# A rewritten issue order for a one-core attention and two-layer MoE kernel

## The chip, the cores and the metric

The kernel runs on one core of a Trainium2 chip. The metric is the device time of one execution in microseconds; the value used for comparison is the median of several runs. The profile comes from one execution of its own, whose span (first to last instruction) is a little shorter than its device time.

## The reference

The computation has three stages, all in float32:

```
attention: B=2, H=8, S=768, D=64; bucket = 6 sign bits of x @ proj (64x6)
  scores = (q @ k.T) / 8 where the buckets of q and k agree, else -1e9
  attn   = softmax(scores);  x = attn @ v, heads side by side -> 1536 x 512
MoE 1:  h = x @ w_in (512x2048);  g = s * relu(h)^2 + b;  x = g @ w_out (2048x512)
MoE 2:  a = x @ w1, b = x @ w2 (512x1024 each);  h = (a * b) @ w3;  out = h @ w_out
```

## The kernel before

Every float32 operand is split into a high and a low part of a faster format, so each product is three matrix multiplications (high x high, low x high, high x low). Weights are brought in as 64-bit words and converted by six steps each, `conv0` to `conv5` (lines 257 to 271): `conv0`, `conv1` and `conv3` on VectorE, `conv2` and `conv4` on ScalarE or GpSimd, `conv5` on GpSimd or VectorE.

Attention works on 16 heads, each in three units of 256 query rows. A unit is two `score` operations (line 529, four matmuls each), for each a `max` on VectorE (line 543) and an `exp` on ScalarE (line 551), three `turn` operations that transpose the result on TensorE (line 565), a split of each transposed piece into high and low parts (`hi` on ScalarE line 603, `lo` on VectorE line 607; for the middle piece `out`, `phi`, `plo` on ScalarE and GpSimd, lines 586 to 597), and three `pv` operations (lines 571 and 572). Per head two `bits` operations (line 492) and `mask` operations (line 510) build the bucket operands, and several small DMAs move halves of the operands between partitions (`mq_d` for the first head, line 477). The first head's second score operation group needs the landed `mq_d`.

MoE 1 runs in two batches: as soon as batch 0's attention is done its `h` and `o` products (line 759) are interleaved with the attention of batch 1, then batch 1's own products follow. The second batch reads its converted weights back from DRAM (`again_wi`, `again_wo`, line 747). While MoE 1 runs, the last two matrices of MoE 2 are multiplied together (`fold`, line 1162). MoE 2 forms its two products by a seven-product scheme (p1 to p7 per block, line 759; `cadd`, `c1`, line 1132 and 1137, combine them on VectorE and ScalarE), multiplies them (`times`, line 1187), splits the result (`abh` on ScalarE line 1190, `cl` on VectorE or GpSimd line 1191) and multiplies by the folded matrix (`share`, line 1203). Twelve output tiles are copied (`ya`, `yv`) and written out.

The order of all this is not left to loops. The program first describes 3773 operations in a `Plan` (each with one or more ways to be done on some engine, and with the tiles it reads and writes) and then issues them in an order written out as a string. `emit` takes three constants: `ORDER` names, two letters each, which operation is issued next; `WAYS` gives for each of 509 operations that can run on two or three engines which one it uses; `PLACES` gives for each of 1724 tiles in which of its pool's buffers it lies. Each engine, and the queue of SyncE that issues all DMAs, executes its own operations strictly in the order in which they stand in `ORDER`. A tile that takes over a buffer has to wait until the operations on the tile before it in that buffer are done. The microseconds written at each `plan.op` are not used by `emit`.

```
        for o in self.ops:
            o["engine"], o["us"], o["fn"] = o["ways"][int(next(ways)) if len(o["ways"]) > 1 else 0]
        issued = [
            self.ops[64 * LETTERS.index(ORDER[2 * i]) + LETTERS.index(ORDER[2 * i + 1])] for i in range(len(ORDER) // 2)
        ]
...
        for o in issued:
            o["fn"]()
```

Of the kernel before, what the change touches and what calls it, by code (L numbers as in the profile page):

```python
# [18 lines left out]
B, H, S, D = 2, 8, 768, 64  # L19
# [10 lines left out]
U = 256  # L30
# [29 lines left out]
    "IuYKIzJ+JaIfKAJeIDI3J/JbL/JiI8JyKBI4MAMGJuJjMFKjJfI5JkKCJcKkJgO2MBJvI9KmJwKlIgJhYcKnJ3MHIEJzLAKhMCKoIFJlLBMD"  # L60
    "J0IjKDJmMIIhMELDJ4J1I+JnLCKMJ5JxMJKiLEKHL9KEJ2KIIiKFLfLFIkO4J6KJMKLgKtK4J7KKLiKNJ8KpKuLjKGNPLVI/KyKqKOKLNXJA"
    "LkNVKPYdJBK5LGKrKQMNLhKvK6KRLKK7NQLWKsMOKzMQNWLLK0LPMPKwQGMRNRYLLHMiNSMLMSKxLIMMK1LMMjNTK2MlLNLQNYLXNULlLYMk"
    "K3LpL0LRQIK8LJLqMmLOLmNZLSLrNNYWLuLTNaM3LnLsMnLUMcM4LZLoYXMdM6LvYOYDMTM5MeO5LtLwMXK9MUPAM7LxMYO6MxNbL1MsLyMV"
    "NdM8L2LzYsK+L3NeLaMZYtO/MtNgK/PBNfMWMaNhO7MyN6LbL4O8NcYPMbMzMfMuLcN7MoMgO9MvMpMhYuNiO+PCYvLdMqNGN8YQN9YYNBYw"
    "MrL5NCYRYxMwL6PEN+M0LeNHPDM9NDM1OZNIYSN/M2NnOaNsM+NEOcaUNoTAM/ObNjYeNANFNyOdNtL7NJNkOEQJNuNpPHNKNlNqQROJOeNL"
    "O3OANzQQNmPIOFQKPKOKN0NrPJOLNvPLOGOjRwNwQLX7YZOkNxN1PcOBQMOHYkPMOCQPQNPdPFODOPOfPGQOPePfaVOIOgaWOMPgYlOlONYm"
    "QSRyOQOoRxOOPxOhYaOpN2YnYfOROqOSPWPhOmPyOiQTY0YoQHP0YyOuYpQUPXOnYgYqPNPYOTRzOrYzPRYhacYrY1R7PSN3Y2OvYiPOY8P1"
    "PzY3Y9PPPTY4QXP2R0Y5Y+OwOxY6ZEOsQ0Y7aMN4Y/R6QVOtQYZFOUZAZGaXZBZHOyQZPUQ1PQXrPrZCZMR5ZIadZNPsZDZOPtZPZJQaZQaN"
    "OzR1ZRPmQbQWPVPnPZR2N5ZUPaaOPiR3aePjZVaPPoR4ZWZSPkPpR9ZXOXPbR8QcZcV6ZkZTQ2ZdaQZlQsZYZeZKZZZmaRaYZfQAZLaZPlaS"
    "RTQBaaakZnZgQCafQ3ZhOYasZuagR+P7O0ZoPqahRUP8PuP9P3Q4ZvRVP+ZpZqQ5alZraiZwP4ZsPvP5OVZxa0ZtOWRWYjTCO1QmQtTDPwZz"  # L70
    "amZ0TKTEZyP6ZaRXZ1QnQhQoZ2anQiUqP/aTZ3ZiQdYTatQjQDaoZ9QeZbZ+apa1Z4auSBaqQfavZ5QEaCR/Zja8Z/SCSAajZ6UrZ7TJSDaD"
# [1192 lines left out]
```

## Time and profile before

| what | us |
|---|---|
| median of 3 runs | 741.59 (741.3 to 741.89) |
| the profiled execution: device time | 742.74 |
| the profiled execution: span | 740.9 |
| TensorE busy (PE), weight loads (PEld) | 729.0, 694.6 |
| VectorE (DVE), ScalarE (ACT), GpSimd (POOL) busy | 590.8, 393.2, 297.5 |

The engines are named PE (TensorE, with PEld for its weight loads), DVE (VectorE), ACT (ScalarE), POOL (GpSimd) and SP (SyncE, which issues the DMAs here). Busy time is the sum of an engine's instructions. Matmul ends are modelled, so how long PE was held up is read better from the starts of its instructions than from its busy time.

### The profile page before, as it was taken

Reading aid. Unit: us, or ns where it says so; the run is one execution under the profiler, and the core shown is the slowest. Engines: PE = TensorE matmul, PEld = TensorE weight load, DVE = VectorE, ACT = ScalarE, POOL = GpSimd, SP = SyncE. Lnnn points to the kernel's source line nnn. Section 1 sums busy time; section 2 is a strip of 40 time slices with the busy share of each in tenths; the row PEclk is TensorE's granted clock in tenths of the full one; section 3 lists DMA queues with packets and bytes.
Section 4 is the critical chain, followed back from the end, with each engine's and each line's share of the span. In section 5 each row is a group of like instructions: output and inputs, shape, how many; then the busy total and the mean of one; then the engine's idle time right before and its main releaser. Section 6 shows DMA issues by size and latency. Waiting matters only on the chain.

```text
span 740.9 us, 12707 instructions
## 1 busy us (share of the span) xinstructions
PE 729.0 (98%) x4356; PEld 694.6 (94%) x4356; DVE 590.8 (80%) x1133; ACT 393.2 (53%) x778; POOL 297.5 (40%) x322
## 2 busy tenths in 40 slices
PE   8899999999999999999999999999999999999997
PEld 6889999999999999999999998999998999999996
DVE  7999999999889889999898667665998965664542
ACT  6989989987667667665373432433533312311111
POOL 2698989886565564334230311032125200111000
PEclk9999999999999999999999999999999999999999
DMA  7856557566677477347888996788899998475502
GB/s 217 244 132 175 141 160 194 149 181 171 195 228 236 119 232 255 93 133 254 288 267 298 317 312 242 256 274 290 315 338 315 353 312 261 141 240 186 179 22 86
DMA packets 78592, 163.03 MB, mean 220 GB/s; under 512 B 8896, under 2 KB 46272, under 8 KB 78528
## 3 DMA queue, kind: packets, MB, share of 16 engines
q1 hardware_dynamic: 78528, 162.22, 68.5%
q8 instruction: 35, 0.57, 0.3%
q14 instruction: 29, 0.24, 0.1%
HBM read 103.09 MB, written 41.21 MB: 195 GB/s over the span
## 4 chain that ended last, share of the span: by engine, by line
PE 86%; DVE 7%; DMA 3%; ACT 2%; issue 1%; SPq 0%; DVEq 0%; ACTq 0%
PE x L759 18%; PE h L759 15%; PE p L759 15%; PE y L1203 9%; PE t L565 7%; PE sc L529 7%; PE psw L1162 6%; PE o L571 4%; PE o L572 4%; PE bits L492 2%; DVE sc L543 1%; DVE pt L607 1%; DMA t<-in_qkT 1%; DMA q<-mm 1%; DMA rd<-rq 1%
## 5 line engine op out<-in xcount | busy, mean ns | idle before, releaser
L759 PE MATMUL h<-x,w_wi 128*128 128x384 f32 x768 | 148.1, 338 | 0.0
L759 PE MATMUL x<-g,w_wo 128*128 128x384 f32 x768 | 146.9, 337 | 1.0 <-DVE rl L833 0.9
L759 PEld LDWEIGHTS x<-g,w_wo 128*128 128x128 f32 x768 | 133.6, 188 | 3.6 <-DVE rl L833 1.6
L759 PEld LDWEIGHTS h<-x,w_wi 128*128 128x128 f32 x768 | 133.6, 188 | 2.5 <-DVE pt L607 0.2
L1132 DVE TENSOR_TENSOR c<-c,p 128x384 f32<-128x384 f32 x112 | 60.2, 552 | 57.7 <-PE p L759 54.4
L543 DVE TENSOR_SCALAR_CACHE_REDUCE sc<-sc 128x768 f32<-128x768 f32 x96 | 91.6, 957 | 3.4 <-PE sc L529 2.4
L551 ACT ACTIVATE p<-sc,least 128x768 f32<-128x768 f32 x96 | 86.9, 906 | 11.1 <-DVE sc L543 7.7
L529 PE MATMUL sc<-k,q 128*128 128x384 f32 x384 | 87.0, 347 | 3.0 <-ACT p L551 2.0
L565 PE MATMUL t<-ident,p 128*128 128x128 f32 x576 | 83.9, 273 | 0.2
L759 PE MATMUL p<-x,w 128*128 128x384 f32 x384 | 77.5, 337 | 0.4 <-DVE c L1132 0.3
L571 PE MATMUL o<-pt,vv 128*128 128x256 f32 x288 | 76.9, 295 | 0.1
L572 PE MATMUL o<-pt,vv 128*128 128x256 f32 x288 | 73.1, 282 | 0.0
L565 PEld LDWEIGHTS t<-ident,p 128*128 128x128 f32 x576 | 67.9, 140 | 5.3 <-DVE pt L607 1.5
L759 PEld LDWEIGHTS p<-x,w 128*128 128x128 f32 x384 | 68.0, 188 | 4.5 <-DVE c L1132 1.3
L597 POOL TENSOR_TENSOR pt<-pf,pt 128x512 fp32r<-128x512 f32 x48 | 63.2, 1317 | 21.6 <-ACT pt L593 20.7
L607 DVE TENSOR_TENSOR pt<-t,pt 128x512 fp32r<-128x512 f32 x96 | 65.0, 683 | 6.7 <-ACT pt L603 5.5
L529 PEld LDWEIGHTS sc<-k,q 128*128 128x128 f32 x384 | 64.4, 188 | 5.2 <-ACT p L551 3.0
L603 ACT CAST pt<-t 128x512 fp32r<-128x512 f32 x96 | 56.0, 586 | 16.7 <-PE t L565 7.6
L571 PEld LDWEIGHTS o<-pt,vv 128*128 128x128 f32 x288 | 54.4, 189 | 0.8 <-DVE xf L624 0.3
L572 PEld LDWEIGHTS o<-pt,vv 128*128 128x128 f32 x288 | 54.5, 189 | 0.2
L838 ACT ACTIVATE g<-rl,b_bc 128x384 fp32r<-128x384 f32 x64 | 38.9, 615 | 25.5 <-PE x L759 17.4
L1162 PE MATMUL psw<-w_wo,w_w 128*128 128x512 f32 x192 | 51.6, 394 | 0.0
(263 smaller groups left out, 1271.7 us busy)
## 6 DMA issues: line engine op xcount, KB each, us to landing
w<-kept_s SPq DMA_DIRECT2D x64, 256.0 KB
kept_wo<-w_wo SPq DMA_DIRECT2D x24, 512.0 KB
w_wo<-kept_wo SPq DMA_DIRECT2D x24, 512.0 KB
w<-kept_a SPq DMA_DIRECT2D x48, 256.0 KB
raw_wi<-in_w_in SPq DMA_DIRECT2D x16, 512.0 KB
raw_wo<-in_w_out SPq DMA_DIRECT2D x16, 512.0 KB
kept_wi<-w_wi SPq DMA_DIRECT2D x16, 512.0 KB
raw_w_a<-in_w SPq DMA_DIRECT2D x16, 512.0 KB
```

The costliest lines, as they stand in the source:

```text
L529: nc.tensor.matmul(sc()[:, i, :HALF], x[:, t], y[:, i * HALF : (i + 1) * HALF], start=st, stop=not st)
L543: lambda j=j, sc=sc: nc.vector.tensor_scalar(sc()[:, :, :HALF], sc()[:, :, :HALF], OUT, None, ALU.min, ALU.min, accum_out=least()[:, j : j ...
L551: lambda j=j, k=k, sc=sc: nc.scalar.activation(ps[j](), sc()[:, :, :HALF], AF.Exp, bias=least()[:, j : j + 1], scale=-1.0, accum_out=ssum( ...
L565: nc.tensor.transpose(tp()[:, e, j * P : (j + 1) * P], flat[:, c * P : (c + 1) * P], ident)
L571: nc.tensor.matmul(o()[:, :U], w, pt()[:, 0, e], start=(c == 0), stop=False)
L572: nc.tensor.matmul(o()[:, :U], w, pt()[:, 1, e], start=False, stop=(c == NC - 1))
L597: lambda pf=pf, pt=pt: nc.gpsimd.tensor_tensor(pt()[:, 1], pf(), r32(pt()[:, 0]), ALU.subtract),
L607: lambda tp=tp, pt=pt: nc.vector.tensor_tensor(pt()[:, 1], tp(), r32(pt()[:, 0]), ALU.subtract),
L759: nc.tensor.matmul(ps()[:, :n], x, y, start=(i == 0 and e == 0), stop=(i == len(terms) - 1 and e == 2))
L1132: "cadd", "dve", 0.47, rank, lambda: nc.vector.tensor_tensor(x(out), a(), p(), op), [(ps, 1), *reads], writes
L1162: nc.tensor.matmul(ps(), w3()[:, p, c], wo()[:, q], start=(j == 0 and e == 0), stop=(j == 7 and e == 2))
L1203: nc.tensor.matmul(y(), abt()[:, p, c], wt()[:, q], start=(i == 0 and e == 0), stop=(i == DF2 // P - 1 and e == 2))
```

## The change

Only the three constants change. The operations, their instructions and their inputs stay the same.

```
 ORDER = (
-    "AKAAAFABALAGBmXkAMACBnANADX0AEXsAOAbAWAPAVAcAhAXAfAdAUBoAgAQAeAYAZAjAaBvAiXlBuBpAkBwB0DPAqXmAlBsAmArAnB1BqAs"
...
+    "AKAAALAFBmABAGXkAMACBnADANAEX0XsAOAbAWAVAcAhAPAgBoAdAUAYAQAfAXAeAaAiAZAjXlBuAkBpBvAlAqXmDPAnBwArAmARB0AoAsBs"
...
 WAYS = (
-    "001100100000001101000110111010110010100210000111011100100010001101100001010111011110101010011010011111101110"
...
+    "001100000020001101101111111000110010100210100111011100100010001101100011010111011110101010011000011111001110"
...
 PLACES = (
-    "ACBDACBACBABACBCABCABCACBACBACBACABCBABCABBCABCABCACBACBACBABCABCABCABCABCABABACCABBACACBBCABACACBCBAABCCBAB"
...
+    "CADBAABCCABABCACBACBACBACBABCABCACBABCBACBBACABCABCBACABCABCBACBACABCABCACACBBCAABCBCACABCABBACCABBACCABA"
...
```

Decoded, 3399 of the 3773 entries of `ORDER` name another operation than before, mostly one that stood a few entries away; of PE's 1317 operations 823 stand at another position of PE's own order. 136 operations go to another engine: DVE has 1020 operations (1023 before), ACT 684 (680), POOL 315 (316). 995 of 1724 tiles lie in another buffer. The orders that the prediction speaks of are these (`x -> y` is issue order on that engine):

```
SP, first 11 issues: the same operations in the same order, mq_d the 11th
DVE, start     before: split_l, qh, mask, mask, mk, conv0, ...   after: split_l, mask, qh, mask, conv0, ... (mk to ACT; one ql from ACT to POOL)
PE, start      before: score1, bits, score0, bits, warm2, ...    after: score1, score0, warm2, bits, bits, ...
DVE, unit 8/9  before: flip, conv0(w_out piece 2), max(unit 8), lo, lo, gather, max(9), mask, max(9), lo
               after:  flip, max(unit 8), lo, lo, gather, max(9), mask, max(9), conv0(w_out piece 2), lo
SP, batch 1's first w_out piece (w_wo_1_0_0, needed first by PE operation x_0_2_1)
               before: raw_wo2, save_wo, save_t, raw_w3, again_wo(piece 3), again_wo(piece 0)
               after:  again_wo(piece 0), raw_wo2, save_wo2, raw_w3, again_wo(piece 3), save_t
DVE, first blocks of MoE 2
               before: cadd u2, cl, conv5(s2), cadd u3, x1l, times     after: conv5(s2), cadd u2, cadd u3, conv5(s4), cl, times
PE, MoE 1, fq 2  before: h(2_1_3) third and fourth part, x_2_0_0      after: ... x_2_0_1, h(2_1_3) fourth part, score, x_2_0_1, x_2_0_0
POOL, same place before: conv5(w_in piece 0 of the last quarter) behind plo and norm    after: that conv5 ahead of plo
PE, whole run: a turn directly behind a turn 20 times before, 27 times after
last cl of the kernel (block 3, left): on DVE before, on POOL after; 5 share operations on PE between the last
               product part of the scheme and the share that reads it
```

## Rows read from the trace of the kernel before

**Rows 1.** The page, its first line and the PE line of section 1.
```profile
span 740.9 us, 12707 instructions
...
PE 729.0 (98%) x4356; PEld 694.6 (94%) x4356; DVE 590.8 (80%) x1133; ACT 393.2 (53%) x778; POOL 297.5 (40%) x322
```

**Rows 2.** Busy time by stretch: length, each engine's busy us, clock, DMA share.
```profile
16.00:27.00 11.00, 8.59 (x52) 7.05 (x52) 10.76 (x21) 9.55 (x20) 4.11 (x4) 1.00 0.62 162
...
60.00:100.00 40.00, 39.97 (x299) 38.77 (x297) 38.01 (x81) 36.41 (x79) 37.57 (x47) 1.00 0.60 153
100.00:140.00 40.00, 39.85 (x291) 38.00 (x290) 37.76 (x81) 37.12 (x78) 35.88 (x43) 1.00 0.62 174
```

**Rows 3.** Waits of PE over the whole run: total us, times, longest.
```profile
PE sc L529 <- ACT p L551: 2.0, 2, 1.2
...
PE x L759 <- DVE rl L833: 0.9, 1, 0.9
```

**Rows 4.** The chain of waits in order of time: start, us, instructions.
```profile
414.74 2.10 PE h L759 x12
```

**Rows 5.** Timeline of PE at the start: start, us, instruction, idle before.
```profile
16.25 0.59 PE L529 MATMUL sc<-k,q 128*128 128x384 f32 x2 [0.39 <-DMA q<-mm]
```

**Rows 6.** Timeline of DVE at the start.
```profile
16.24 1.26 DVE L510 TENSOR_SCALAR mm<-bits,thr,sgn 128x384 fp32r<-128x384 f32 x2 [0.36 <-DMA q<-mm]
```

**Rows 7.** Timeline of PE from 49 to 57 us.
```profile
49.97 0.60 PE L565 MATMUL t<-ident,p 128*128 128x128 f32 x4
50.32 0.36 PE L571 MATMUL o<-pt,vv 128*128 128x256 f32 x1
...
50.88 1.04 PE L565 MATMUL t<-ident,p 128*128 128x128 f32 x8
51.67 0.96 PE L529 MATMUL sc<-k,q 128*128 128x384 f32 x4
53.65 0.41 PE L492 MATMUL bits<-q,pj_h 128*128 128x384 f32 x1 [1.02 <-DVE pt L607]
```

**Rows 8.** Timeline of DVE at the same place.
```profile
50.15 1.88 DVE L260 TENSOR_SCALAR raw_wo<-raw_wo 128x512 int32<-128x512 uint32 x1
```

**Rows 9.** Timeline of POOL at the same place.
```profile
49.91 1.83 POOL L375 TENSOR_TENSOR k<-t,q 128x768 fp32r<-128x768 f32 x1
```

**Rows 10.** Line 260 by instruction: ns least, median, most; first and last start.
```profile
L260 DVE TENSOR_SCALAR raw_wo<-raw_wo x24: 366/423/1878, 41.5 to 426.3; 128x512 int32<-128x512 uint32 x24
```

**Rows 11.** Timeline of PE from 386 to 391 us.
```profile
387.10 2.79 PE L759 MATMUL h<-x,w_wi 128*128 128x384 f32 x15
390.76 0.41 PE L759 MATMUL x<-g,w_wo 128*128 128x384 f32 x1 [0.87 <-DVE rl L833]
```

**Rows 12.** Timeline of SP's DMA queue from 372 to 391 us.
```profile
382.47 0.80 SPq L747 DMA_DIRECT2D w_wo<-kept_wo  x2
```

**Rows 13.** Timeline of PE from 560 to 580 us.
```profile
571.32 0.68 PE L759 MATMUL p<-x,w 128*128 128x384 f32 x3
572.28 0.79 PE L759 MATMUL p<-x,w 128*128 128x384 f32 x3 [0.28 <-DVE c L1132]
```

**Rows 14.** Timeline of DVE at the same place.
```profile
570.26 1.51 DVE L271 TENSOR_TENSOR w_w_s<-raw_w_a,w_w_s 128x512 fp32r<-128x512 f32 x1
571.69 0.54 DVE L1132 TENSOR_TENSOR c<-c,p 128x384 f32<-128x384 f32 x1
```

**Rows 15.** Timeline of DVE and PE from 303 to 308 us.
```profile
303.59 1.80 DVE L261 SCALAR_TENSOR_TENSOR raw_wi<-raw_wi 128x512 int32<-128x512 int32 x1
...
304.70 1.73 PE L759 MATMUL h<-x,w_wi 128*128 128x384 f32 x9
...
306.57 0.79 PE L759 MATMUL x<-g,w_wo 128*128 128x384 f32 x3
```

**Rows 16.** Timeline of DVE and PE near the end.
```profile
725.48 0.56 DVE L1191 TENSOR_TENSOR abt_(1, 0)_8821<-c,abt_(1, 0)_8821 128x384 fp32r<-128x384 f32 x1 [0.63 <-ACT abt_(1, 0)_8821 L1190]
...
726.60 0.84 PE L1203 MATMUL y<-whl,abt_(1, 0)_8821 128*128 128x512 f32 x3
```

More of the change, by code (lines that the diff above doesn't have):

```diff
@@ new lines @@
+    "BqX1ApASXtAxXnX2AyX3BrA/AzBtA8A0BAAtBxA2AuB1A9EeATBBByAvA+BUXuX4A3BRBzXoAwDRXvBVA1BGX5DYA4BWAHDSA5DXXpXwDTEg"
+    "BSXqB2A6DVBHA7XxBTB3X8BCDaX6BDDZB5DWEfBIDUBLB4BJBEBbB6BMBFXyCTBcBNB7BgCUBXBhBKDcX9CWDbCVBiDQBOX+YMCABYYUCXBd"
+    "B8BPGICyCBX/BZCYBeCFBQCzBaC1B9YABfC0EhC2BjCZCGCLEnEiDfB+C3EoCHCdBkDiDgCeCoL8ElDdCCCMCiDHDhBlCDCNB/EmCODjEjCa"
+    "CEYBYNCICbCfYCEqD0DkEpEkC4D1C8CgCJD3CjCKD2DIGKCcCPCkChC9DJDeD4ClErC5DKDBCmC+EJC6D5EsCnDpC/YEEKDCEMDqC7DDGLEL"
+    "DACpDlGMCqENDrCrDuDmDEGTD+DnDvGREvCQDFGSDwEOGNL+DGD6EwD/CsCREyDsGOExDoGPEzDLCSD7EDDtHYYVE0DxEtD8GUFMGQEEEADy"
@@ new lines @@
+    "ETFNGVCtFPEUEBDzEPCwCuFQEYFOD9DMECEFEQGWFrFEHaFRCxEREGCvE5DNEVFsEHFuEZEWEIE1E6EaESFtE+FvHbEXE2EbHcHhFFE/E3FS"
+    "GJFwGZHiFGFAFWEcDOGaJCGcFXFHEuHdEdGbHfGdE7E4GuE8HgFTHkHeGXFbAJGeFUGYE9HlFBHjGvFcFhF6FYGxFCFdGwGAFZFxFDF1GyFI"
+    "HDF2JEHmFiGzFVJDFaHEF3HZFeFyF4HGFfFjFzFkF7GfFgGjHFJFF8F0GBF5FJJLGkHHF9GgJGGoF+GhHpFlGpF/G0HIGCGqJMGiFKGDHqG9"
+    "G1FLHsGlKSG2JHHrGmHtG4HnIGG5YFGnJIFmHuGEJJIHHoGrFpJOG+IJJKJNFqGsHSAIFnG/G6H+HNJPFoIIGtHJG7IKG3HOIlKUHKJQHzYG"
+    "ILG8GFHAHLHPH0IoGGImHBHQH4HTHvHCInHUHMKVHRH/HwIpIQKWKbH5HVIRHxJTHWH6IMIqGHNMKXJUKTKZIbH1JRIAJWJVHXIBI6H2KaHy"
@@ new lines @@
+    "JXKcIVINKdJoJSXzKYJYH3IOYHH7KfIWI0JpISIvH8JrITKeIXIwJqH9IrIcICIPYIIUIdJsIsYJO3IYIxIeJ9NOIZItJZI1IyIaKgJdJtJ+"
+    "IuYKIzJaI7I2KAJeIfJ/I3IDYcL/JbJiI4KBJuJjMFMAKjJfMGI5JyKCJkJcKkJgMBJvKmI8JwKlI9IEJhKnIgJ3JzO2LAKhMHIhMCIFKoJl"
+    "LBMDJ0JmKDMEMIJ4J1LDIjJnLCMJKMJ5I+JxIiLEKHK4IkKEJ2KiKILfKFLFO4J6KJL9LgKtMKJ7LVLiKKKuJ8KpKNLjKGNPI/KyKqKOKLJA"
+    "NWLkNVYdKPJBK5NXKrLGKQMNKvLhKRNQK6LKK7MOKsKzMQLLK0MPLPKwQGLWNRMRYDLHMiYLMLNSMSKxMMLXK1LINTLMMjMlK2NYLNLQLlLY"
+    "NUMkK3LpL0LRQIK8LJLqMmLOLmNZLSLrYWLuLTM3NaLnLsMnNNMTLUM4McLZYXLoMdM6K9LvMeLtM5O5LwMXL1K+LxMUM7MxK/MYNdLyMVO6"
@@ new lines @@
+    "M8MsL2LzL3YsNeMtNgPBMZYOMWO/NfYtLaMaO7NhNbN6LbL4MyO8LdYPMbPANcMzMfMuN7MoLcMgO9LeMpYuMhMvNiO+YvMqNGPCYwN9L5N8"
+    "YQNBYYL6MrNCYRYxMwM0N+NDNHM9PEM1YSOZNIPDN/NnM2NsOaNEaUM+OcRxNoM/ObNjQJOdNAL7NFQQNtNJQPYeNkOERwNyNuNpPHNKNlNq"
+    "OJOeNLOANzNmPIOFQKPKOKN0NrPJOLN1NvPLOjQRNwOGQLOkNxPFPcQMOBOHYkPMOCQNPdOPYZODQSOITAQOPeYlaVPfOQOlOROoaWOSOMOm"
+    "PgOfQUYmOgQTPxYaONN2OhOpYnOOPhPWPyOTPGOiYfOnOqacOuP0YoRyYyYpOrPXYgY0YqY1PYN3RzPNYrPRYhR5YzY2PSR7OvYiY3P1PzXr"
+    "Y8Y9POOwR0OxQXOsPPY4Y+X7QYP2Y/aMPTZEQHZAY5N4R6Q0QZOtPUPrQ1Y6ZFOyaXZGZBPQOUZMPsY7PVZCPtN5ZNZHZDZOOVZIQVZPZJQW"
@@ new lines @@
+    "R1ZQQaZKZROzPmR2PZadPnR3aNO0QbPoZUPaR8ZSPiZVPpPjR4ZWQcPkZXZTZcQ2aOZdPbZeOXaPZLZfOYZYPlZZQ3aQZkaeaRQAaYZlQBZm"
+    "aSaZZnQCakZgRTaaafZhZuZoZvasQsagP7UrRUP3ahP8ZwTCQ4PqPuOWZpP9alZqP4aiQ5ZrP5P+a0ZsR+RVZxaTO1RWZyR9PvZtQmajQhat"
+    "PwTDZzZ0ZiamTJZ1QiRXTEP6Z2QnQtP/ZaZ3QdanQoQjV6QDYjaoZ9TKQeZ4R/UqapQfZ5YTRYZbZ+auaCaDa1avZjZ/QEa2SBQuRoaEaqQv"
+    "SCaAZ6awSDa8SWQFRJTLQkZ7aBQgZ8SESASXaHUsQ+SFaxaFQ/aIaya3aJaGbERAaKYbTFRBabaLRDRKQ6TGQlSGa4THa9QpQ7a5TISZQqQ8"
+    "a6REbMRLQrRMRdbNa+ReQwbORFSYa/bPc8bFQ9bQbATBRCRfTMbRSubBSabSRZbCRiRaSvRGbUc0RjbVSwRkbWQxbXbTQySrRbTObYQzbcTN"
@@ new lines @@
+    "RHRpbdV8bGSLRgbZbHbeRIbabfSsRNUtSbbkRcbIU1bgblUzbbSMRhc9bmRqSNbhRrbnUuRlbobDSHTPSObpSQSITRbiSJbsRObqTSbtSRRP"
+    "b0RmTQTTbuRnV7b1c1RsStSSb2SKbrarbJSPc+b3bjTUc2b4bvbKb5c3SlTVSTbwb8RtdESmbxb9U0c/b+SnbyRuSgb6bzb/Shc4ScSiUNb7"
+    "SddAcEcASeSjcFSUTWcGcBcHSVdFcMcITmcNdBcJcORRdCc5UxSfUyUvRSdDUOS1RvdMSkS2U2RQcPUwSodGU3S6c6a7TuS7dHc7UPcRS8S3"
+    "dccSTvSpSxS4cTSycQcUTwcbcVU4TxdNazdOcccdSqdIceUQdJcfSzcWdKV9TbTycXWFTccYV+dUURcCcZcKTgcaTzS0cDS5ThcLS9dPTXTi"
+    "S+cgU5TYS/U7USdddQchdeTdcldRcmTZTecidfcndgcjTndSTackcoU8T4UiTfT5cpcqU9dVcrTodWTpcsT6ctdXdLT9cudkVQWEdYT+bLcv"
@@ new lines @@
+    "U6WDcwT/U+VRdZTjdacxU/TkcydhWBczT7fcT0WCV/T1d0WAVAd1dld2TlVSUDd8T2d3UEWGdiVTTqd4UFdmUXdsVod5dnUYT3d6fdUcfeWI"
+    "UTdodbT8UGd9VUdpUdUAUUffWHd+UeVVdqd/UVeEeAVlUZTreBUBeFUaUjeGeCUCVaVmUHUWVbeHeDVFd7eIUbdtVGUfeJVKUkUgfgeMUlVL"
+    "dueNVHeOVMVnVIePUheUVpeQWLWJUIUmeKeReVULWMVBfkTsecdTTtVCdjeWeSeLedWNeTeeUMVDeXdvUJefeYdwekegeZWOdxehVfeadyWP"
+    "VEVqVJVNebfsVgeldrflVcUnVhesVOemfmfhVWVPenfiVXeteieueoVYVdf0WoWQepe5fnejevftUoWrWpewUpe6e0exWgVZfoe1fufpe2Ws"
+    "Wqe7fqe8Whe3e9fvf8e+e4UKVef1VvWif2e/WjVwV0fwf3fAfxfDf4XHVxfyV1fBVygEf5V2VifjfEfCVjf6fFXIeyVreqfGezgMVsfNf7er"
@@ new lines @@
+    "XJfOdzf9fzfPVtWtXKVkfHW9fIWKfQWVgFfJf+WWVugGf/fKgNgHfLfRVzfMV3WXXLWaV4WYWRWbfSXMWcfTgIfUWSfXV5XcWTfYgJgOfZfa"
+    "gKgPfVXdgUgAWyWUfWWzgBWZfbWdgCWuWetSgcW0WfW3gQWvWkgdW4W1WwgegRXegfXfW+W5WxgSgggkfrghglgVgitNXRgmgjXSW2tTXTW6"
+    "gWgnW/XUW7XAXNgoW8gsXOgpgLWlgtgXXPXWWmgugYXXgvgqXBXYXQgZgrXVgwXZtUg0gagxXag8Xbgyg1XgtVg9g2gzgDg3tWt6hEXCg4hF"
+    "g5Wng+g6hGXhtOXDhHXig7XFg/hIXGhUhJXjhAhVhKhBhWXEtPhcpEhCpFhMpYhDhXtht7hNhLhYhOtQhZhPiEt8hdhQtihetRhmtjhfhRgT"
+    "hniFpGhghopHhpwBhhpIhqhrtqhshSpJhipZpKhthjpLhkpaprhuiGhlpbhwiHhThah1hvhxwDpcwFhyhbh2wCh6wGh7pdh3pehzwEh8pNps"
@@ L125 @@
+    "001010110000001111011101110110100010101010001111011110001001001001100110111111001111111200001110111001100000"
+    "110110100110010100000001100011100001010110000001100100100000001110000100000101000011001000000001011011001001"
+    "001001011111110001001011001101101001011101001010001001011111001010000111101001000000010111000011000110000010"
+    "00010001100110110000101010000010010110011010100010111111001110101100001111001"
 )
 PLACES = (
[L127 removed]
@@ new lines @@
+    "BAABABAABAABBAABABAAABBABAABABBBAABBBAABAABBABADBEFCDADBAECFDAABFCDEFBFACBDEFBECDFBADEBACEFDBAACFDBEACADBECF"
+    "DAABBACACBBACACBBAAABABABABABBBABABABABAIEFLMEDNIJHGBACJDAJCMGIHFBLMNKHEMIKLIFHKKLJBGKBMGNLEMNGBELBACBABCBBA"
+    "ABABABHDGGHCHECDGBDFHBADGBFHEBCDGAACDBCBACABCDIFHJEBBHJEDFGCGDFICBHADHIBAEJFHJCIFABDEBAJIDGHCHJABDGIGBCAFEHD"
+    "FGBDCEGFHEACDBAHECDAGECDBHAFEGDCBFEGADHBFGECDABHGECAHFBDABABABABABABABBABABBBAAABABABABABBBAABABABABABBABABA"
+    "ABAABABAABAABABAABABBAABBBABAABBBABBABAABABBAABBABBAABABABBADAECCBBECEAFCFBEFDECCDBADEFABCEAABAABBAABABB"
```

133 lines of the change are left out of this document (42 added, 91 removed).

## The prediction

> **What bounds the kernel now.** I read the page first. PE is busy 729.0 of 740.9 us [rows 1], and its clock is granted in full in every stretch read, so PE's instruction stream is the bound and there are some 12 us of idle time to win at most. The next view is the busy time by stretch [rows 2]: from 60 to 140 PE idles 0.03 + 0.15 us, but DVE stands at 38.01 and 37.76 of 40 and POOL at 37.57 and 35.88. The second engine has next to no slack there; the reader is to keep this for the rivals. Third come PE's own waits [rows 3]: few are large. Two score products behind ScalarE's `exp` (2.0 together) and one `x` behind `rl` (0.9) lead, and most of the rest of PE's idle time is scattered in pieces of some 0.1 us where it goes from one tile to the next. Fourth, the chain [rows 4]: `h` x12 in 2.10 us. As products of 128x384 stand back to back there, that gives 2.10/12 = 0.174 us per product, with which I size a stall: from the start of one run of products, count x 0.174 must bring the next start; what lies above it is lost.
>
> The end needs no view of its own beyond the timeline [rows 16]: the last products are PE's and only copies and a write follow, in both orders the same.
>
> The sum is made against the profiled execution, 742.74 us (740.9 span and 1.9 around it). It lies 1.15 above the median of 741.59; the difference that I work out is carried to the median unchanged.
>
> **The change part by part.** No instruction is added or removed on PE, so only its stalls, and what it pays between tiles, can change.
>
> *Start.* SP's first eleven issues stay; the eleventh, `mq_d`, gates PE at 16.25 and DVE at 16.24 [rows 5, 6]: both idle until `q` is there. From 16 to 27 DVE is then 10.76 of 11 busy [rows 2] with the same work in another sequence up to the second head's first `max`. One `mk` off DVE and one `ql` off ScalarE fall before the landing. I take 0.
>
> *Piece 2 of w_out's conversion at unit 8.* PE issues four score products at 51.67; 4 x 0.174 = 0.70 brings 52.37; the next product starts at 53.65 [rows 7], 1.28 late, and the row names a `lo` (line 607). Behind that stands `conv0` on DVE, 1.88 us from 50.15 [rows 8], where the same instruction takes 0.423 in the median of 24 [rows 10]: 1.46 too long, while POOL's line 375 runs from 49.91 for 1.83 us and ends within 0.3 of it [rows 9]. DVE did not do anything for longer; it stood until POOL was through. The new order puts this `conv0` behind both `max` and both `lo` of these units, so PE's product no longer has it ahead. The `conv0` still costs DVE 0.42 somewhere near, which PE may feel: -1.28 + 0.43 = -0.85. Bounds: -1.28 if nothing of it reaches PE, 0 if it meets a POOL instruction again. The nearest row for the value is the median of line 260.
>
> The Trainium skill has this as a rule (SBUF — State Buffer, section "Who interferes with whom"): VectorE and GpSimd share one pair of ports, whichever instruction takes the pair first holds it throughout, and the other stands; "Issue order, not op shape, decides who blocks." The trace agrees here, 1.88 against 0.423. By the rule, an operation's traced time belongs to its neighbour on POOL as much as to itself, and a reordering draws these neighbours anew; with that the term here would be anything from -1.28 to 0. It also speaks against the change as a whole, which is rival B and C below, worked out from rows alone.
>
> *Batch 1's first w_out piece.* From 387.10 fifteen products need 15 x 0.174 = 2.61, to 389.71; the `x` product starts at 390.76 [rows 11], 1.05 late. The view names `rl` [rows 3, 11]. But the weights that this `x` reads come by `again_wo`, which SP issued at 382.47 behind other stores [rows 12], eight microseconds before the product's start, as the last of a row of transfers. In the new order this load stands ahead of `raw_wo2`, `save_wo2`, `raw_w3` and `save_t`, and is issued before these block it; SP holds for none of the others a load that PE reads first. -1.05. If `rl` was the releaser after all, a part of this stays; bounds -1.05 and 0. I take -1.05, because DVE's `rl` had no long instruction ahead of it in that stretch.
>
> *First blocks of MoE 2.* From 571.32 three products need 0.52, to 571.84; the next starts at 572.28 [rows 13], 0.44 late behind `cadd u3`, which DVE could begin only at 571.69, after a `conv5` of 1.51 us (570.26) [rows 14]. The new order has `cadd u2` and `u3` behind one another, with that `conv5` ahead of both and another behind. -0.44. Bounds: -0.44, and +0.5 if the `conv5` ahead is as long again and now delays both.
>
> *MoE 1, fq 2.* From 304.70 nine products need 1.57, to 306.27; the `x` product starts at 306.57 [rows 15], 0.30 late, with a `conv1` of 1.80 us from 303.59 on DVE before it. In the new order another `x` product and a score of four products (4 x 0.174 = 0.70) stand in between, more than the wait. -0.30; bounds -0.30 and 0.
>
> *Turns.* A `turn` directly behind a `turn` occurs 27 times and not 20. What that costs is read from one pair of rows: from the `turn` at 49.97 to the `pv` behind it 0.35 us, from the two turns at 50.88 (x8) to the score at 51.67 0.79 [rows 7], 0.79 - 2 x 0.35 = 0.09 for each. 7 x 0.09 = +0.6. Bounds 0 and 7 x 0.2.
>
> *Engines.* 136 operations change engine, but the counts hardly move: DVE loses 3 operations of 1023, POOL 1, ScalarE gains 4. At 590.8 us / 1133 instructions = 0.52 us each [rows 1] DVE is lighter by some 1.6 us; at PE 0. The last `cl` goes from DVE (0.56, 725.48 [rows 16]) to POOL, which I take at twice that; five shares, 0.7 us each (0.84 for one run of three [rows 16], its overlapping tail left off), stand between it and its reader and cover the extra. 0; bound +0.5, if POOL is as much slower and nothing covers it. All other steps are moved by a few places inside stretches where PE does not wait now: 0, which their cover must bear out. That is the weak item: the cover is DVE's slack, 1.99 + 2.24 = 4.23 us in 60 to 140 [rows 2].
>
> Sum: -0.85 - 1.05 - 0.44 - 0.30 + 0.6 = -2.0. Profiled 742.74 - 2.0 = 740.7; median 741.59 - 2.0 = 739.6.
>
> **The rivals.** *B, the waits are re-drawn and nothing is won.* Each long DVE instruction (1.88, 1.80, 1.51 [rows 8, 15, 14]) is so by its POOL neighbour, and the new order has as many instructions of both kinds. PE pays for such a one only where the operation it delays is next in PE's queue; in this trace three of them cost it 1.28 + 0.44 + 0.30. If one or two new ones fall so, at 1.28 each, the sum is -0.7 to +0.6: 741.5 in the middle, 740.9 to 742.2. For it: POOL is busy 94% and 90% in 60 to 140, so that any instruction of DVE moved there meets one. Against it: PE loses only 0.18 us in these 80 us, although the same lottery was played there.
>
> *C, slower: DVE becomes the bound in the attention of batch 0.* Between 60 and 140 DVE has 4.23 us left. Three lock waits of 1.46 more than now (1.88 - 0.42) are 4.4 and use it up; from the third on each one reaches PE as at 53.65, 1.28, since a late `lo` or `max` there has no later cover. -2.0 + 3 x 1.28 = +1.8: 743.4; five of them give 746. It decides from the third long wait in that stretch. For it: 3399 entries change, so nearly every DVE instruction there gets another neighbour on POOL. Against it: PE's reserve of independent `h` and weight work is absent only in batch 0, and some long waits that are there now leave as well.
>
> *D, a larger gain.* The two score waits behind `exp`, 2.0 together [rows 3], lie in the first 28 us, where the order of ScalarE changes as well. If they go too: -2.0 - 2.0 = -4.0, and with bits of the scattered rest -4.3: 737.3. Against it: in that stretch DVE is 98% busy [rows 2] and feeds these `exp`.
>
> **How the numbers follow.** The smallest change that a measurement of this kernel can tell from none is about 0.2%, 1.5 us: 740.1 to 743.1. The forecast, A, 739.6, has 0.45; its own range, with the bounds of the terms, is 738.3 to 741.0, of which 0.33 lies below 740.1 and 0.12 within. B has 0.22 (0.16 within, 0.06 slower, where a second long wait is worse than the one removed), C 0.21, all slower, D 0.12, all faster. Faster 0.33 + 0.12 = 0.45; same 0.12 + 0.16 = 0.28; slower 0.06 + 0.21 = 0.27. The range reaches from below D's value, 736.0, to C with four long waits, -2.0 + 4 x 1.28 = +3.1, to 744.8; beyond lie some 0.05 of D and 0.08 of C.
>
> **What would show it right or wrong.** In the profile after: PE's wait of `bits` for a `lo` near 53 us gone, and line 260's longest no longer beside it; the `again_wo` of that piece issued well before 382 and no `x` wait of 0.9 in PE's list (if the load is early and the wait stays, `rl` was the releaser and that step is wrong); no wait at the `p` product near 572; the 2.0 for `sc` behind `exp` still there (gone: D). Long instructions of lines 260, 261, 271 should still be there at other places; how many of them have a PE wait behind them decides between A and B, and PE's idle time in 60 to 140, now 0.18, decides C: over 3 us there would be C. PE's first product after `mq_d` must again stand near 16.25. The prediction is wrong at its root if PE's starts are later with no stall in its list, as the same products at the same clock are all that the sum counts on.

## The result, and the profile after

The changed kernel takes 747.14 us (median of 6 runs, 745.42 to 749.04), the kernel before 741.44 (6 runs): ratio 1.0077, 95% interval 1.0056 to 1.0097. It is 5.7 us slower, where 2.0 us faster was forecast, and it lies above the upper end of the range (744.8). The profiled execution took 747.37 us; its span is 4.7 us longer than before [rows 1].

The page of the new kernel, first line and PE line:

```profile
span 745.6 us, 12704 instructions
...
PE 731.8 (98%) x4356; PEld 695.1 (93%) x4356; DVE 592.9 (80%) x1130; ACT 394.8 (53%) x782; POOL 297.9 (40%) x321
```

VectorE has three instructions fewer and is still 2.1 us busier. With each instruction taken at the median of its kind (same line and shape in both traces), its work sums to 639.9 us before and 639.5 after. The instructions that stand more than 0.2 us above that median add 17.1 us before and 19.4 after.

Busy time by stretch (columns as in [rows 2]), with one more stretch at the start:

```profile
13.50:20.00 6.50, 4.46 (x22) 4.08 (x21) 4.24 (x8) 2.03 (x5) 2.85 (x3) 0.74 0.59 128
16.00:27.00 11.00, 9.99 (x51) 8.71 (x51) 10.35 (x19) 6.79 (x13) 6.37 (x6) 0.85 0.53 143
60.00:100.00 40.00, 40.00 (x296) 38.63 (x296) 38.39 (x83) 36.63 (x79) 35.82 (x45) 1.00 0.56 150
100.00:140.00 40.00, 39.37 (x290) 37.66 (x289) 38.03 (x79) 36.53 (x77) 34.59 (x42) 1.00 0.68 186
340.00:380.00 40.00, 39.13 (x235) 38.16 (x234) 35.21 (x64) 20.69 (x41) 10.12 (x11) 1.00 0.69 227
```

From 60 to 140 PE idles 0.63 us, 0.18 before [rows 2]: the forecast's rival C, with its price in this stretch, is not what happened. From 340 to 380 it idles 0.87 us, and from 13.5 to 20 its clock is granted only 0.74 on the mean.

Waits of PE over the whole run:

```profile
PE sc L529 <- DMA q<-mm: 2.0, 1, 2.0
...
PE h L759 <- DVE rl L833: 0.8, 2, 0.5
PE sc L529 <- ACT p L551: 0.8, 2, 0.5
PE o L571 <- DVE xf L624: 0.7, 2, 0.5
PE t L565 <- DVE mm L510: 0.6, 1, 0.6
PE x L759 <- DVE rl L833: 0.5, 1, 0.5
PE t L565 <- DVE pt L607: 0.4, 1, 0.4
...
```

No wait that the view puts down to VectorE is as long as the 0.9 of before [rows 3] or the 1.02 at 53.65 [rows 7], but there are more of them, each 0.2 to 0.8 us. Sizing every wait by the prediction's rule (from one start to the next, less count x nominal) gives the account of the 4.7 us. Before, the waits from 0.2 us up that stand after 28 us and are gone now sum to 4.7 (1.29 at 53.65, 1.04 at 390.76, 0.44 at 572.28, 0.31 at 306.57, the other six 0.2 to 0.4). The nineteen new ones sum to 8.2. Changes of tile rose by 0.8 in sum, the start is 0.4 later at 28 us: -4.7 + 8.2 + 0.8 + 0.4 = 4.7, with waits under 0.2 left out.

One execution alone could mislead. But seven of the nineteen, at 109.42, 143.99, 242.87, 359.83, 367.73, 528.80 and 566.29 us and 0.5 to 0.8 us each, stand again in the trace of e8_startB, a kernel below that has the new order from 29 us on: at 106.54, 140.81, 242.02, 359.61, 367.50, 529.09 and 566.91 us, 0.5 to 1.2 us each. In the trace of the new kernel each of the seven ends 0.04 to 0.05 us behind the end of a VectorE instruction. These belong to the order. From the waits of PE in e8_startB:

```profile
PE x L759 <- DVE rl L833: 1.0, 1, 1.0
PE h L759 <- DVE rl L833: 0.8, 2, 0.5
PE t L565 <- DVE mm L510: 0.8, 2, 0.4
...
PE x L759 <- DVE acc L853: 0.3, 1, 0.3
```

The nineteen have three shapes. **A VectorE operation that PE waits for stands behind another one that could have stood behind it**: 4.8 us of the 8.2 (of this, 0.6 in two waits is behind ScalarE or has no clear releaser). VectorE and PE of the new kernel at 142 us:

```profile
142.40 0.95 DVE L543 TENSOR_SCALAR_CACHE_REDUCE sc<-sc 128x768 f32<-128x768 f32 x1
...
143.27 0.67 DVE L510 TENSOR_SCALAR mm<-bits,thr,sgn 128x384 fp32r<-128x384 f32 x1
...
143.99 0.66 PE L565 MATMUL t<-ident,p 128*128 128x128 f32 x4 [0.61 <-DVE mm L510]
```

PE's transpose needs the buffer that `mask` reads; `mask` could have begun at 141.8, when its `bits` were done, and stands behind a `max` of 0.95 us. **The operation ahead is lengthened**, mostly beside GpSimd: 2.4 us in four waits. At 564 us, VectorE, GpSimd and PE:

```profile
563.80 1.42 POOL L270 TENSOR_TENSOR w_w_a<-raw_w_a,w_w_a 128x512 fp32r<-128x512 f32 x1 [2.64 <-DMA w<-kept_s]
...
563.97 1.81 DVE L1092 TENSOR_TENSOR raw_w_a<-raw_w_a,raw_w_a 128x512 f32<-128x512 f32 x1
565.70 1.20 DVE L1132 TENSOR_TENSOR c<-c,p 128x384 f32<-128x384 f32 x2
...
566.29 0.97 PE L759 MATMUL p<-x,w 128*128 128x384 f32 x4 [0.34 <-DVE c L1132]
```

A sum that takes 0.69 us at 569.16 takes 1.81 here, and the `cadd` behind it frees PE's buffer 0.5 us late. **VectorE stops at the landing of a load**: 1.0 us in two waits. At 356 us:

```profile
355.99 0.62 DVE L842 SCALAR_TENSOR_TENSOR g<-rl,b_bc,g 128x384 fp32r<-128x384 f32 x1
358.30 0.43 DVE L260 TENSOR_SCALAR raw_w_a<-raw_w_a 128x512 int32<-128x512 uint32 x1 [1.68 <-DMA raw_w_a<-in_w]
358.64 0.61 DVE L842 SCALAR_TENSOR_TENSOR g<-rl,b_bc,g 128x384 fp32r<-128x384 f32 x1
359.17 0.61 DVE L833 SCALAR_TENSOR_TENSOR rl<-h,sw,rl 128x384 f32<-128x384 f32 x1
...
359.83 0.97 PE L759 MATMUL x<-g,w_wo 128*128 128x384 f32 x4 [0.54 <-DVE rl L833]
```

The `rl` that PE waits for was ready at 357.25; VectorE's queue was held by a weight conversion whose data had not landed. The chain of waits that ended last points the same way. Three of its long pieces after 28 us are transfers of weights; the chain of before has no transfer of weights there (its one long transfer after 28 us is the small `rd`, 4.31 us at 97.19):

```profile
351.19 7.08 DMA raw_w_a<-in_w
...
413.76 5.96 DMA raw_wo<-in_wo
...
570.60 4.56 DMA raw_w_a<-in_w
```

### The profile page after: what moved, and what is told of

Its sections match the earlier page's. It is cut to its first block, busy times and chain, and to the rows that moved or that the text cites. A ratio compares the mean times of both kernels' runs of the same rounds, so it can differ in the third digit from the quotient of the medians.

```text
span 745.6 us, 12704 instructions
## 1 busy us (share of the span) xinstructions
PE 731.8 (98%) x4356; PEld 695.1 (93%) x4356; DVE 592.9 (80%) x1130; ACT 394.8 (53%) x782; POOL 297.9 (40%) x321
## 4 chain that ended last, share of the span: by engine, by line
PE 82%; DVE 8%; DMA 5%; issue 1%; POOL 1%; ACT 1%; SPq 1%; DVEq 0%; ACTq 0%; POOLq 0%
PE x L759 15%; PE h L759 15%; PE p L759 14%; PE y L1203 8%; PE sc L529 7%; PE t L565 7%; PE psw L1162 6%; PE o L571 4%; PE o L572 4%; DMA raw_w_a<-in_w 2%; PE bits L492 2%; DMA t<-in_qkT 1%; DMA q<-mm 1%; DVE sc L543 1%; DVE pt L607 1%
## 5 line engine op out<-in xcount | busy, mean ns | idle before, releaser
L597 POOL TENSOR_TENSOR pt<-pf,pt 128x512 fp32r<-128x512 f32 x48 | 64.7, 1348 | 28.4 <-ACT pt L593 24.9
L828 ACT ACTIVATE rl<-h 128x384 f32<-128x384 f32 x64 | 31.0, 490 | 44.7 <-PE h L759 31.5
```

What stands on the lines that cost most here:

```text
L597: lambda pf=pf, pt=pt: nc.gpsimd.tensor_tensor(pt()[:, 1], pf(), r32(pt()[:, 0]), ALU.subtract),
```

## The experiments

Each compares with the kernel before, run beside it on the same chip. The times are medians in us, followed by the ratio to the kernel before and its 95% interval. The edits are in ORDER, WAYS and PLACES and are shown decoded.

**Order alone and engines alone.** The new ORDER and PLACES with the WAYS of before, and the reverse:

```
 e1_order: ORDER, PLACES of the new kernel;  WAYS of before
 e2_ways:  ORDER, PLACES of before;          WAYS of the new kernel
```

> The new order and the new buffers, with every operation on the engine that it had before: only the written order is changed. Theory T (the order itself: an operation of VectorE that PE's next instruction waits for stands one place too far back in VectorE's queue): nearly all of the loss is here, 4 to 6 us over the kernel before (745.5 to 747.5). Rival L (the loss is made by the 136 operations that went to another engine, and by the waits between VectorE and GpSimd that they bring): at most 1.5 us over the kernel before (741.4 to 743).

> The order and the buffers of before, with the 136 operations on their new engines: only the engines are changed. Theory T: the smaller part, 0 to 2 us over before (741.4 to 743.5), as operations of another duration now stand in an order that was not written for them. Rival L: 3 us or more over before (744.5 to 747).

Order alone 746.91 (before 740.57; ratio 1.0089, 1.0075 to 1.0103), engines alone 746.96 (1.0085, 1.0071 to 1.0100). Each costs what both together cost. Neither theory had that: the 136 engine moves cost 6.4 us by themselves, but they add nothing to the new order. That an order fits the engines for which it was written would explain why either change alone loses. It does not explain why the new order with its own engines loses as much; that stays open. e1_order also carries the new buffers, and no run takes order and buffers apart.

**First part and rest.**

```
 e3_first: new order for the first 1016 operations (162 us), then that of before
 e4_rest:  order of before for the first 1016 operations, then the new one
```

> The first 1016 operations of the new order (to about 162 us: the attention of batch 0, with 14 of the 136 engine moves), then all others in the order of before. Theory T: PE's lag after 160 us in the two traces differs by 2.1 us, so 2.1 us over before, 743.5. If the loss were the start alone (PE's wait for mq_d and the halved clock from 16 to 19 us), the excess would be the same 0.4 us as at 28 us: 741.8. Rival L: 14 moves make nearly nothing, 741.4 to 742.

> The first 1016 operations in the order of before, all others in the new one with 122 of the 136 engine moves. Theory T: 4.7 - 2.1 = 2.6 us over before, 744. Rival L: all of the loss, 746 to 747. Rival start (only the first 28 us count): all of the gains that were forecast for 306, 390 and 572 us stay, -1.8, so 739.6.

First part 742.77 (1.0023, 1.0012 to 1.0035), 2.2 us over before, as read from the traces; rest 745.35 (1.0060, 1.0048 to 1.0072), 4.8 us where 2.6 was expected. The loss is spread over the run, and the start alone is not it. The two parts sum to more than the whole; each spliced kernel also has a seam between two orders, which no run prices.

**The four terms of the forecast, alone, in the kernel before.**

```
-conv0(w_out 2), max(8), lo, lo, gather, max(9), mask, max(9)    DVE
+max(8), lo, lo, gather, max(9), mask, max(9), conv0(w_out 2)
-again_wo(2), save_wo2, ..., raw_w3, again_wo(3), again_wo(0)    SP
+again_wo(2), again_wo(0), save_wo2, ..., raw_w3, again_wo(3)
-lo(pt_43_0), square(rl_2_1_2)                                   DVE
+square(rl_2_1_2), lo(pt_43_0)
-conv5(s2), cadd u3                                              DVE
+cadd u3, conv5(s2)
```

> The kernel before with the four gains of the prediction alone, by four moves in ORDER and nothing else: w_out's conv0 of piece 2 behind the max operations of unit 9; batch 1's again_wo of piece 0 issued right behind that of piece 2; square of rl_2_1_2 ahead of lo of pt_43_0; conv5 of s2 behind cadd u3. Theory T (the terms were right, what was missed lies elsewhere in the new order): -0.85 - 1.05 - 0.44 - 0.30 = -2.6 us against before, 738 (737.5 to 739). Rival R (each wait that is taken away comes back at the next place): within 0.8 us of before, 740 to 741.4.

742.14 (before 740.37; 1.0026, 1.0009 to 1.0043): slower, both theories missed. The four executions of the twelve that took 744.17 to 746.12 are those with a mean granted clock of 0.997 to 0.998; the other eight, at 0.999 or 1.0, have a median of 740.9. The traced one is among the eight, so what the four lost is not shown. The terms were then taken apart: three moves without the one in SP's queue, and that one alone:

> The kernel before with three of the four named moves, without that of again_wo: conv0 behind the max operations of unit 9, square of rl_2_1_2 ahead of lo of pt_43_0, conv5 of s2 behind cadd u3. Theory T: -0.85 - 0.30 - 0.44 = -1.6, so 738.8, with a spread as in the kernel before. Rival R (the wait comes back behind the next lengthened operation): within 0.7 of before, 739.8 to 741.

> The kernel before with the again_wo of piece 0 issued ten microseconds earlier, alone. Theory T (the wait at 390 us is that load's, and earlier is free): -1.05, 739.3. Rival D (the earlier 512 KB crowd out a load that VectorE waits for, and the wait moves to another product, as 0.94 us at 384 in the kernel with all four moves): 740 to 742, with runs 3 us apart.

Three moves: 739.85 against 740.83 (0.9988, 0.9979 to 0.9996), the one kernel here whose interval lies below that of before, by 0.9 us and not 1.6, at the edge of rival R's range. The load alone: 742.28 (1.0020, 1.0008 to 1.0032), 1.5 us slower where -1.05 was forecast, with executions 4.4 us apart. Its trace, of an execution of 741.82 (VectorE, GpSimd, PE at 382 us), shows a new wait at another product:

```profile
381.88 2.07 POOL L892 TENSOR_TENSOR acc<-acc,acc 128x768 f32<-128x768 f32 x1 [4.63 <-DVE x L867]
...
382.15 2.34 DVE L261 SCALAR_TENSOR_TENSOR raw_wo<-raw_wo 128x512 int32<-128x512 int32 x1
...
384.42 1.13 DVE L833 SCALAR_TENSOR_TENSOR rl<-h,sw,rl 128x384 f32<-128x384 f32 x2
...
385.08 1.14 PE L759 MATMUL h<-x,w_wi 128*128 128x384 f32 x5 [0.85 <-DVE rl L833]
```

The conversion's second step, 0.69 us elsewhere, took 2.34 beside a GpSimd instruction that began 0.27 us ahead of it, and PE came 1.02 late at 385.08. The Trainium skill's rule on the shared pair of ports (SBUF — State Buffer, section "Who interferes with whom") fits these rows: the later one stood until the earlier was through. GpSimd's ended at 383.95, VectorE's at 384.49.

**Eleven waits repaired in the new kernel, and a random reordering of before.**

```
 e6_repair, DVE, new order with 11 moves, as
-norm(xf_12), lo(pt_18_0)      -max(27), mask(mm_10)      -conv1, add(acc_0)
+lo(pt_18_0), norm(xf_12)      +mask(mm_10), max(27)      +add(acc_0), conv1
 e7_random, DVE, order of before: 240 neighbouring pairs swapped at random
```

> The new kernel with eleven moves on VectorE alone, each of which takes the operation that PE's late instruction waited for out from behind another one (lo of pt_18_0, mask of mm_10, gl of g_1_0_2, square of rl_1_1_1, rl_3_1_3 and rl_3_2_1, two adds, three cadds). These waits are 5.1 us in the profile of the new kernel. Theory T (VectorE's queue order is what costs): 4 to 5 us less than the new kernel's 747.1, so 742 to 743. Rival L (VectorE's operations are longer beside GpSimd's and it is simply later everywhere): at most 1.5 us less, 745.5 or more.

> The kernel before with 240 of VectorE's neighbouring pairs swapped, drawn at random among those that may be swapped (the new order reverses 248 of the 1022 pairs of neighbours of before); engines and buffers as before. Theory F (the order of before fits the measured times so closely that any other order of VectorE loses): 3 to 7 us over before, 744 to 748. Rival S (the loss is particular to the moves of the change): at most 1.5 us over before.

Repaired: 747.15 (743.40 to 747.72; 1.0072, 1.0051 to 1.0094), no gain in the median. Its executions fall into two groups, two at 743.4 to 743.5 and four at 746.8 to 747.7. The traced one took 743.54 and does show most of these waits gone, but 1.01 us at 242.59, 0.84 at 530.89 and 0.83 at 141.56 had come at the next product behind the one repaired, and 0.66 at 209.37 was new. What the four at 747 lost is not traced, so that returning waits undid the repair is argued and not shown. Random: 793.41 (1.0706), far beyond the 3 to 7 that were expected. The change reverses some 250 of VectorE's 1022 neighbouring pairs, about as many as were swapped here, and loses a tenth as much (5.7 against 53). It moves other engines and buffers as well, so the comparison is rough.

**The start.** PE and the landing of `mq_d` in the new kernel:

```profile
13.62 0.59 PE L529 MATMUL sc<-k,q 128*128 128x384 f32 x2
16.25 2.26 PE L529 MATMUL sc<-k,q 128*128 128x384 f32 x6 [2.04 <-DMA q<-mm]
18.31 1.55 PE L565 MATMUL t<-ident,p 128*128 128x128 f32 x8
```

The landing is where it was [rows 5], but the warm products (matmuls whose results nobody uses) that filled the time ahead of it now stand elsewhere. PE idles 2.04 us, and the granted clock is at the lower level (1.2 GHz) for 3.4 us from 16.0: six products take 2.06 us and not 6 x 0.174 = 1.04.

```
 e8_startB:  order of before for the first 138 operations (29 us), then the new one
 e11_startA: new order for the first 138 operations, then that of before
```

> The new kernel with its first 138 operations (to 29 us) in the order of before, where twelve warm products fill PE's time ahead of the landing of mq_d. Theory C (mq_d lands between 14.7 and 16.2 us; when it is late PE idles 2 us in the new order, its clock is halved from 16 to 19 us, and about 4 us lie between such runs): the runs of the new order at 747 to 749 disappear, the median is 745 to 745.5 and all runs lie within 2 us. Rival (the start is covered by VectorE, 0.4 us at 28 us): median 746.7, spread over 3 us as in the new kernel.

> The kernel before with its first 138 operations (to 29 us) in the new order. Theory C: two groups of runs, 740.5 to 741.5 where mq_d lands early and 3 to 4 us above that where it is late; median 741.5 to 743. Rival (start covered): 740.8, spread as in the kernel before.

Old start 746.07 (before 740.83; 1.0069, 1.0056 to 1.0082), with executions still 3.3 us apart: 5.2 us over before where the new kernel has 5.7, so by the medians the start is 0.5 to 1 us of the loss, and the intervals overlap. New start 744.61 (1.0049, 1.0034 to 1.0064), 3.8 us over before and above the 741.5 to 743 expected, yet with the clock at full in its traced execution:

```profile
13.50:20.00 6.50, 5.55 (x33) 4.31 (x32) 5.81 (x12) 5.02 (x11) 3.36 (x4) 1.00 0.68 156
```

There `mq_d` had landed a microsecond earlier, PE waited 0.34 for it, and lost 1.56 us at 38.39 to a small DMA of the third head. The new kernel has no such wait there, so this kernel does not price the new start alone. The halved clock of the new kernel was traced in one execution, whose mean clock is 0.998. One more of its six is below 0.999 (0.997, at 746.92); the other four lie on both sides of these two, from 745.42 to 749.04. The median does not rest on it.

**Queues that stop at a landing.** The profiled execution of e8_startB (748.32, the longest of its six) traces one such stop through three engines to PE (GpSimd, ScalarE, VectorE, PE):

```profile
179.96 0.59 POOL L369 TENSOR_SCALAR vv<-tv 128x384 fp32r<-128x384 f32 x1 [4.15 <-DMA tv<-in_vl]
...
182.43 0.41 ACT L688 CAST x<-xf 128x256 fp32r<-128x256 f32 x1 [2.07 <-POOL xf L674]
...
184.40 0.69 DVE L607 TENSOR_TENSOR pt<-t,pt 128x512 fp32r<-128x512 f32 x1 [2.11 <-ACT pt L603]
...
186.69 0.36 PE L571 MATMUL o<-pt,vv 128*128 128x256 f32 x1 [1.33 <-DVE xf L624]
```

In e4_rest, with the same order there, GpSimd stopped 1.91 us at the same instruction and PE lost 0.29. The load is issued right behind 512 KB of weights in the new order, and ahead of them before. Two kernels test this, one without such stops in the new order, one with this stop put into the kernel before:

```
 e12_loads, new order: vh, vl of vv_11 behind norm, phi, plo on POOL; seven conv0 and one
            conv1 on DVE, one norm on POOL moved behind the next one to eight operations
 e13_latev, SP, order of before
-load(tv_11), mk, rr, raw_wi(1_2)
+mk, rr, raw_wi(1_2), load(tv_11)
```

> The new kernel with eleven moves of operations that stood waiting for a landing at the head of VectorE's or GpSimd's queue: vh and vl of vv_11 behind plo of pt_31_1, seven conv0 or conv1 behind the next square, add, max or conv5, norm of xf_18 behind split_h. Theory D (in the new order users stand too close behind their loads, so the queue stops at the landing, and landings differ between runs): 1 to 2.5 us less than the new kernel, 744.6 to 746, and runs within 2 us. Rival T (only the order among ready operations counts): 746.5 to 747.5.

> The kernel before with one move in SyncE's queue: the load of tv_11 behind that of raw_wi_0_1_2 (512 KB) and not three issues ahead of it; its first user on GpSimd stays where it was. Theory D: GpSimd stops at vh of vv_11 for 1.5 us or more, and with it norm, xh on ScalarE and lo on VectorE, so that PE waits 0.5 to 1.5 us: 741.4 to 742.4. Rival: hidden, 740.5 to 741.

Without the stops 745.51 (1.0072, 1.0052 to 1.0092): the median is 1.6 us lower, but the interval does not tell it from the new kernel, and its executions lie 5.6 us apart where 2 was expected. The waits at 359.83 and their like are gone from its trace and so are the weights from its chain after 28 us. With the stop 741.48 against 741.20 (1.0010, 0.9998 to 1.0021); GpSimd did stop, and PE did not wait:

```profile
174.02 0.52 POOL L369 TENSOR_SCALAR vv<-tv 128x384 fp32r<-128x384 f32 x1 [1.64 <-DMA tv<-in_vl]
```

Here a stop of 1.64 us was hidden; one of 4.15, in the new order, was not.

**All repairs together, and more moves of the kind that helped.**

```
 e15_all:  start of before + the 11 moves of e6 + ten of e12
 e14_best: the 3 moves of e9 + 5 on DVE: wsum behind square (536 us), add ahead of max (316),
           conv1 behind lo (133), gather ahead of r (103), x1l behind cadd (572)
```

> The new kernel with all repairs together: its first 29 us in the order of before, the eleven moves on VectorE and ten of the moves behind landings. If the loss is the sum of these single waits: 1.1 for the start, 2 to 4 for the others, so 742 to 744. If every repair makes its own new wait: 745.5 to 747.

> The kernel before with the three moves that made it faster (conv0 behind unit 9, square of rl_2_1_2, conv5 of s2) and five more of the same kind, taken from the waits that were left: wsum of raw_w12_0_1_a12 behind the square of rl_3_3_3 (0.79), add of acc_0 ahead of max of unit 47 (0.41), conv1 of w_out piece 1 behind lo of pt_24_2 (0.33), gather of xf_13 ahead of r of unit 17 (0.37), x1l behind the third cadd (0.51). Theory T: 1 to 2 us under the kernel with three moves, 738 to 739. Rival R (waits come back behind the next operation): 739.5 to 741.

All repairs: 744.97 (1.0054, 1.0042 to 1.0066), between the two expectations: 3.8 us over its own before where the new kernel lost 5.7, with intervals that overlap. Eight moves: 740.74 against 741.20 (0.9997, 0.9988 to 1.0007), no gain over three. The eight contain the three, so the 0.9 us of the three is not confirmed. In the trace of the eight the five waits are gone, and waits of 0.3 to 0.6 us at 106.39, 134.38 and 318.81 and two shorter ones at 107.88 and 108.69 are new.

## Why the prediction was wrong

The step that failed is the last term of the sum, the one put at nothing: "All other steps are moved by a few places inside stretches where PE does not wait now: 0, which their cover must bear out." Their cover did not: nineteen new waits of 0.2 to 0.8 us, 8.2 us together, stand in stretches where PE lost next to nothing before. I had counted VectorE's slack over 80 us; what matters is the margin of each single operation before PE's next instruction needs its buffer, and PE waits for a late one whatever the sum. That these were 4.8 us order, 2.4 neighbours on GpSimd and 1.0 landings is read from one execution, though seven of the waits stand again in e8_startB. The term for the engines failed as well: the 136 moves were put at 0 because the counts hardly change, and alone they cost 6.4 us (e2_ways), as the order alone costs 6.3 (e1_order). Why the two do not add is not shown.

*conv0 at unit 8, -0.85.* Right in its mechanism, and by the trace a little larger. The score and the `bits` behind it in the new kernel, timeline of PE:

```profile
53.42 0.95 PE L529 MATMUL sc<-k,q 128*128 128x384 f32 x4
54.21 0.33 PE L492 MATMUL bits<-q,pj_h 128*128 128x384 f32 x1
```

0.79 lies between the starts, where 1.98 stood [rows 7]; in e9_three it is 0.78. By the traces this move carries the gain of e9_three, but it was not run alone. Line 260 on these tiles is no longer held so long (at most 965 ns, 1878 before [rows 10]):

```profile
L260 DVE TENSOR_SCALAR raw_wo<-raw_wo x24: 409/422/965, 43.1 to 429.8; 128x512 int32<-128x512 uint32 x24
```

*306 and 572, -0.30 and -0.44.* The waits went, but in e9_three 0.41 came at 316.78 and 0.51 at 572.13 in their place: nothing is left of the two. Another 0.79 came at 536.84. In the new kernel 0.51 came at 566.29.

*again_wo, -1.05.* Right about what PE waited for, wrong in counting it as a gain of the order. The kernel e13_latev has the order of before at this place, and PE did not wait there (PE, then VectorE):

```profile
387.04 2.78 PE L759 MATMUL h<-x,w_wi 128*128 128x384 f32 x15
389.67 1.20 PE L759 MATMUL x<-g,w_wo 128*128 128x384 f32 x6
...
390.02 0.60 DVE L833 SCALAR_TENSOR_TENSOR rl<-h,sw,rl 128x384 f32<-128x384 f32 x1
```

The `x` product starts ahead of the `rl` that the view of before names as releaser, so it does not need that `rl`. It needs the load. In the trace of before the load is issued at 382.84, its last part lands at 390.62 (by the updates of its semaphore), and PE starts at 390.76. In e11_startA, the one other trace with this wait, the landing is at 391.92 and the start at 392.06. In the five others that have this order of SP there (e2_ways, e3_first, e9_three, e13_latev, e14_best) the load lands 5.0 to 7.3 us after its issue, 7.8 in these two, and PE does not wait. So the wait belongs to some executions and not to the order. The profiled execution of before was one of them, and stood 1.15 us above the median. Up to this product the trace of e13_latev runs within 0.1 us of it, and it ends 1.0 us sooner (741.76 against 742.74). Carrying this term to the median unchanged was the mistake. Without it the account of the new kernel's waits reads -3.7 + 8.2 + 0.8 + 0.4 = 5.7, the difference of the medians; from one execution each, a fit that close is in part luck. What makes the load land late stays open. Issued early and alone, the load cost 1.5 us (e10_dma); its trace shows a conversion behind it held beside a long GpSimd instruction.

*Start, 0.* 0.4 in the profiled execution, where PE idled 2.04 us and ran at a halved clock that no rival had; by the medians of e8_startB 0.5 to 1.

*Turns, +0.6.* All changes of tile together measure +0.8; the turns alone were not sized, so the agreement may be luck.

*The last `cl`, 0.* Right: it takes 1.01 us on GpSimd and ends at 732.43, and its reader on PE starts at 732.68 with no stall.

*The range of A.* The bounds of the terms together give -3.1 to +2.4 us, 738.5 to 744.0, and not the 738.3 to 741.0 that the prediction states. The measured 747.1 lies outside both.

*The rivals.* B was nearest in its mechanism (waits re-drawn; seen in e5, e6, e14) but its price, one or two waits of 1.28 us, was too small by a factor of three to six against 8.2. C had the sign; its place, 60 to 140 us, is refuted by the 0.63 us that PE idles there. D's two score waits shrank from 2.0 to 0.8, and 2.0 for `mq_d` came ahead of them.

*Left open.* All repairs together won about 2 of the 5.7 us, not clear of the noise. The traces show waits that come back behind the next operation; that these hold the rest is argued, and I have not found a local edit that ends them.

## What to carry to other kernels

Where one engine is the bound and every other feeds it from an in-order queue, price a reordering by the margin of each release and not by the busy time left in the stretch: list the operations that free a buffer for the bound engine's next instruction, and see what each stands behind in the new queue. A wait seen in one profiled execution is a gain only if other executions have it too: the waits of before at 53.65, 306.57 and 572.28 stand again in e10_dma, e11_startA and e13_latev, the one at 390.76, of these, only in e11_startA. A move that takes a wait away counts only once the next product behind it has been looked at: of eight such moves here three brought 0.9 us, and with five more nothing was left that could be told from before. Judge an order and its engine assignment together, for each of the two alone lost as much as both.

## What was not expected of the hardware

A load's landing differs between executions of the same order: `mq_d`, with the same ten issues ahead of it, let VectorE's `mask` begin at 16.24 us in the profiles of before and after, at 16.15 in e13_latev, and at 14.6 to 15.6 in the other fourteen. With the start of before this shifts PE by 1.3 us at 40 us (e4_rest against before). The load for the `x` product at 390.76 landed 5.0 to 7.8 us after its issue in seven traces with the same order of SP there.

In the new kernel PE's clock fell to its lower level at 16.0 us, within an idle time of PE from 14.2 to 16.25, and stayed there for 3.4 us. It did so in one other trace, e7_random, at 618.2 us and for 3.4 us, just after PE had stood still for 1.85 us up to 617.92.
